# Weights in natural row order, attention output packed whole from a tile by heads, and the clamp on VectorE

## The chip, the cores and the metric

The kernel runs on one core of a Trainium2 chip. The metric is the device time of one execution in microseconds (us). The time before was 523.95 us, the median of three runs (523.85 to 524.45). Engines: PE is TensorE, DVE is VectorE, ACT is ScalarE, POOL is GpSimd; SPq and ACTq are the sequencers of SyncE and ScalarE when they issue transfers. PEld is PE's loading of weights.

A ratio below is the mean time of one kernel's runs over the mean of the other's runs of the same rounds, with a 95% interval. It is therefore not quite the ratio of the medians that are quoted beside it.

## The reference

```python
# attention: B=4, H=8, S=768, D=48
f = 1 / (1 + exp(-f_logit))
for t in range(S):
    state = f[:, :, t, :, None] * state + einsum('bhd,bhe->bhde', k[:, :, t], v[:, :, t])
    y[:, :, t] = einsum('bhd,bhde->bhe', q[:, :, t], state)
x = y.transpose(0, 2, 1, 3).reshape(3072, 384)
# maxout feed-forward: 384 -> 768 -> 384
out = maximum(maximum(x @ w1, x @ w2), x @ w3) @ w_out
```

The four weight matrices come in as float64. The kernel reads them as pairs of 32-bit words and rounds them to fp32 itself.

## The kernel before

The attention goes in 24 units, each one chunk of 64 tokens of two batches, 128 tokens in all. A unit is called chunk *u* here. Four chunks make a group of 512 tokens, and there are six groups. While PE works on the attention of one group, the feed-forward network (FFN) of the group before is slipped in step by step: 18 steps of six matmuls with w1, w2 and w3, then four steps with `w_out`. In the first group, the FFN steps also carry the rounding of the weights, 24 pieces of 128 columns. One rounding is a chain over three engines:

```python
def round_begin(n, h):
    ...
    nc.scalar.activation(top, hi, AF.Abs)                       # ACT
    nc.gpsimd.tensor_scalar(top, top, HI_MIN, None, op0=max)    # POOL: the clamp
    nc.vector.tensor_scalar(top, top, 3, 0x3FFFFFF8, ...)       # DVE: shift and mask
    nc.scalar.activation(rest, lo, AF.Copy, scale=2.0 ** -29)   # ACT
    nc.gpsimd.tensor_tensor(top, top, rest, op=ALU.add)         # POOL
def round_end(n, h):
    nc.vector.scalar_tensor_tensor(w, hi, 0xC0000000, top, ...) # DVE: combine
```

Heads are 48 wide, so 384 features do not fall on 128 partitions head by head. The kernel before puts 48 rows of each of the first six heads at partitions 0 and 64, and fills the 16 rows behind each with a quarter of the last two heads. The weights' rows must be in the same odd order. That costs four transfers for a weight piece:

```python
def in_rows(dst, src):              # two parts of 48 rows and two of 16
    ...
for h in range(2):                  # at the start: 3 pieces x 2 halves x 4 parts = 24 transfers
    for n in range(3):
        load_weight(n, (h,), one)
...
finish(2, xT); pack(2, xT)          # six copies out of PSUM, then six transfers of `last`
load(GRP); load_v(GRP)              # inputs of chunk 4
pairs(3)
for r in rounds[0:3]: round_begin(*r)
values(3)
for r in rounds[0:3]: round_end(*r)
...
finish(3, xT); pack(3, xT, both)
```

`both` means that the transfers alternate between the queues of SP and ACT; otherwise SP issues them.

Of the kernel before, what the change touches and what calls it, by code (L numbers as in the profile page):

```python
# [9 lines left out]
FP32 = mybir.dt.float32  # L10
I32 = mybir.dt.int32
U32 = mybir.dt.uint32
AF = mybir.ActivationFunctionType
ALU = mybir.AluOpType
# [40 lines left out]
def kernel(  # L55
# [28 lines left out]



# [4 lines left out]
    def fast():  # L91
        ctx = ExitStack()
        with ctx:
# [91 lines left out]
            def in_rows(dst, src):  # L185
                parts = []
                for par in range(2):
                    p0 = par * DP
                    parts.append((dst[p0:p0 + D], src[0:NK * 2 * D].rearrange(
                        "(kt par p) c -> par p kt c", kt=NK, par=2)[par]))  # L190
                    parts.append((dst[p0 + D:p0 + DP], src[NK * 2 * D:].rearrange(
                        "(par kt p) c -> par p kt c", par=2, kt=NK)[par]))
                return parts
# [3 lines left out]
            pieces = [(w_in[i][:, :, c0:c0 + 256], src[:, c0:c0 + 256], in_rows)  # L197
                      for c0 in range(0, DFF, 256) for i, src in enumerate((moe_w1, moe_w2, moe_w3))]
            pieces += [(w_out[:, 2 * n:2 * n + 2, :], moe_w_out[n * 256:(n + 1) * 256, :],
                        lambda dst, src: [(dst, src.rearrange("(j p) c -> p j c", p=128))]) for n in range(3)]  # L200
            RAW = 6
            raw = {}

            def half(x, n, h, words=1):
                return x[:, :, h * 128 * words:(h + 1) * 128 * words] if n < 9 else x[:, h:h + 1, :]

            def load_weight(n, halves=(0, 1), queues=both):
                if n >= len(pieces):
                    return
                dst, src, split = pieces[n]  # L210
                words = 1
                if src.dtype != FP32:
                    words = 2
                    a, w = dst.shape[1:]
                    if n not in raw:
                        raw[n] = work.tile([128, 2 * 768], U32, name="raw", bufs=RAW)
                    dst, src = raw[n].rearrange("p (a c) -> p a c", a=a), src.bitcast(U32)
                if len(halves) == 1:
                    c = slice(halves[0] * 128 * words, (halves[0] + 1) * 128 * words)
                    dst, src = dst[:, :, c], src[:, c]  # L220
                for i, (d, s) in enumerate(split(dst, src)):
                    queues[i // 2].dma_start(out=d, in_=s)  # L222

            halfway = {}
            N = 384

            def round_begin(n, h):
                if n in raw:
                    a = pieces[n][0].shape[1]
                    words = half(raw[n].rearrange("p (a c) -> p a c", a=a), n, h, 2)  # L230
                    words = words.rearrange("p a (c two) -> p a c two", two=2)
                    lo, hi = words[:, :, :, 0], words[:, :, :, 1]
                    shape = "p (a c) -> p a c"
                    a = lo.shape[1]



                    top = work.tile([128, N], U32, name="top_bits", bufs=4).rearrange(shape, a=a)
                    nc.scalar.activation(top.bitcast(FP32), hi.bitcast(FP32), AF.Abs)  # L239
                    nc.gpsimd.tensor_scalar(top.bitcast(FP32), top.bitcast(FP32), HI_MIN, None, op0=ALU.max)  # L240
                    nc.vector.tensor_scalar(top, top, 3, 0x3FFFFFF8, op0=ALU.logical_shift_left, op1=ALU.bitwise_and)  # L241

                    rest = work.tile([128, N], U32, name="rest_bits", bufs=3).rearrange(shape, a=a)
                    nc.scalar.activation(rest, lo, AF.Copy, scale=2.0 ** -29)
                    nc.gpsimd.tensor_tensor(top, top, rest, op=ALU.add)  # L245
                    halfway[n, h] = (top, hi)

            def round_end(n, h):
                if n in raw:
                    top, hi = halfway.pop((n, h))  # L250
                    nc.vector.scalar_tensor_tensor(half(pieces[n][0], n, h).bitcast(U32), hi, 0xC0000000, top,
                                                   op0=ALU.bitwise_and, op1=ALU.bitwise_or)
                if h == 1 and n + RAW < len(pieces):
                    raw.pop(n, None)
                    load_weight(n + RAW)


            rounds = [(3 * (j // 2) + i, j % 2) for j in range(NJ) for i in range(3)]
            rounds += [(9 + j // 2, j % 2) for j in range(NJ)]
# [125 lines left out]
            def finish(u, xT):  # L385
# [10 lines left out]
                xT, last = xT  # L396
                t0 = u % GRP * UT
                for par, a, n in ((0, 0, 2), (1, 1, 1), (0, 1, 1)):
                    i, o = slice(par * DP, (par + n) * DP), slice((par ^ a) * DP, ((par ^ a) + n) * DP)
                    nc.scalar.copy(last[o, t0 + a * C:t0 + (a + 1) * C], y[i, a, NK * C:HP * C])  # L400
                for par, a, n in ((0, 0, 2), (1, 1, 1), (0, 1, 1)):
                    i, o = slice(par * DP, (par + n) * DP), slice((par ^ a) * DP, ((par ^ a) + n) * DP)
                    nc.scalar.copy(xT[o, :, t0 + a * C:t0 + (a + 1) * C],  # L403
                                   y[i, a, 0:NK * C].rearrange("p (h t) -> p h t", h=NK))
                ready.pop(u)

            def pack(u, xT, queues=one):

                slot = u % GRP
                if slot < GRP - 2:  # L410
                    return
                xT, last = xT
                t = slice(0 if slot == GRP - 2 else slot * UT, (slot + 1) * UT)
                for i in range(NK):
                    for par in range(2):
                        p0 = par * DP
                        queues[par].dma_start(out=xT[p0 + D:p0 + DP, i, t],
                                              in_=last[p0 + i * TAIL:p0 + (i + 1) * TAIL, t])


            def ffn(g, xT):
                xT = xT[0]
                hm = work.tile([128, NJ, TOK], FP32, name="hm", bufs=1)
                for j in range(NJ):
                    top = None
                    for i in range(3):
# [10 lines left out]
                        if g == 0:  # L437
                            step = 3 * j + i
                            for r in [3 + step] if step < 12 else [2 * step - 9, 2 * step - 8][:24 - 2 * step + 9]:
                                if r < len(rounds):  # L440
                                    round_end(*rounds[r])
                                if r + 1 < len(rounds):
                                    round_begin(*rounds[r + 1])
# [24 lines left out]
            def new_xT():  # L468
                return work.tile([128, NK, TOK], FP32, name="xT"), work.tile([128, TOK], FP32, name="last")
# [4 lines left out]
            with tc.manual_schedule():  # L474
# [4 lines left out]
                load(2, one, "f")  # L479
                load(2, one, "kq")  # L480
                load_v(1)
                load(3)
                load_v(2)
                load_v(3)
                for h in range(2):
                    for n in range(3):
                        load_weight(n, (h,), one)
# [10 lines left out]
                for u in range(2):  # L498
# [5 lines left out]
                    finish(u, xT)  # L504
# [5 lines left out]
                finish(2, xT)  # L510
                pack(2, xT)
                load(GRP)
                load_v(GRP)
                pairs(3)
                for r in rounds[0:3]:
                    round_begin(*r)
                values(3)
                for r in rounds[0:3]:
                    round_end(*r)
                round_begin(*rounds[3])  # L520

                nc.tensor.transpose(ps_tr.tile([128, 128], FP32, name="tr"), ident, ident)
                finish(3, xT)
                pack(3, xT, both)
                for n in range(3, RAW):
                    load_weight(n)
# [7 lines left out]
                load(GRP + 1)  # L534
                load_v(GRP + 1)
                fill(1)
                for u in range(GRP, NU):
# [3 lines left out]
                    if u > GRP:  # L541
                        finish(u - 1, xT)
                        pack(u - 1, xT)
# [25 lines left out]
                finish(NU - 1, xT)  # L569
                pack(NU - 1, xT)  # L570
# [11 lines left out]
    def general():  # L582
# [5 lines left out]
        with ctx:  # L588
# [53 lines left out]
            def chunk(u, xT):  # L642
# [60 lines left out]
                if c < NCH - 1:  # L703
# [10 lines left out]
                    for par in range(2):  # L714
# [6 lines left out]
                        else:  # L721
                            nc.vector.tensor_copy(new, ds[r, :, e])


                z = work.tile([G, H, D], FP32, name="g_z")
                nc.vector.tensor_tensor(z, y.rearrange("t (h d) -> t h d", d=D), own, op=ALU.add)
                x = work.tile([G, NK, 2, DP], FP32, name="g_x")
                nc.vector.tensor_copy(x[:, :, :, 0:D], z[:, 0:2 * NK].rearrange("t (i par) d -> t i par d", par=2))
                nc.vector.tensor_copy(x[:, :, :, D:DP],
                                      z[:, 2 * NK:].rearrange("t par (i d) -> t i par d", d=TAIL))  # L730
                x = x.rearrange("t i par d -> t (i par d)")
# [75 lines left out]
```

## Time and profile before

| stretch of the span (kernel before) | us | what holds it |
|---|---|---|
| to the first FFN matmul | 56.3 | weights issued in 24 transfers, then the pack |
| first FFN matmul to first `w_out` matmul | 84.8 | roundings through POOL |
| the rest | 381.2 | PE, busy without a gap |
| span | 522.3 | |

A row of the table ends where PE starts something that it could not start earlier. A saving in the third row counts only if it is PE's own. A saving in the first two counts if it shortens what PE waits for. The prediction shows the lines.

### The profile page before, as it was taken

Reading aid. Unit: us, or ns where it says so; the run is one execution under the profiler, and the core shown is the slowest. Engines: PE = TensorE matmul, PEld = TensorE weight load, DVE = VectorE, ACT = ScalarE, POOL = GpSimd, SP = SyncE. Lnnn points to the kernel's source line nnn. Section 1 sums busy time; section 2 is a strip of 40 time slices with the busy share of each in tenths; the row PEclk is TensorE's granted clock in tenths of the full one; section 3 lists DMA queues with packets and bytes.
Section 4 is the critical chain, followed back from the end, with each engine's and each line's share of the span. In section 5 each row is a group of like instructions: output and inputs, shape, how many; then the busy total and the mean of one; then the engine's idle time right before and its main releaser. Section 6 shows DMA issues by size and latency. Waiting matters only on the chain.

```text
span 522.3 us, 10050 instructions
## 1 busy us (share of the span) xinstructions
PE 469.9 (90%) x4067; PEld 252.4 (48%) x4067; DVE 209.8 (40%) x322; ACT 120.9 (23%) x299; POOL 126.8 (24%) x156
## 2 busy tenths in 40 slices
PE   5730679997699999999999999999999999999994
PEld 4630334553365555565454654545655445544452
DVE  7733147675632543523553243556225521021110
ACT  2332132552221231131123122202302210200000
POOL 2124158888622121211220220221021210000000
PEclk9785689997799999999999999999999999999998
DMA  9955998773115660126630146711163001200012
GB/s 131 142 157 105 179 163 114 170 132 44 28 33 73 112 79 1 28 53 87 107 50 10 33 67 107 88 18 28 35 83 72 1 4 23 50 0 0 1 23 45
DMA packets 164456, 34.98 MB, mean 67 GB/s; under 512 B 154800, under 2 KB 161328, under 8 KB 164400
## 3 DMA queue, kind: packets, MB, share of 16 engines
q1 hardware_dynamic: 160848, 31.46, 38.2%
q10 hardware_dynamic: 3552, 2.78, 3.1%
q8 instruction: 34, 0.56, 0.5%
q14 instruction: 22, 0.18, 0.1%
HBM read 28.31 MB, written 4.72 MB: 63 GB/s over the span
## 4 chain that ended last, share of the span: by engine, by line
PE 74%; DMA 7%; SPq 6%; POOL 5%; issue 3%; ACT 2%; DVE 1%; ACTq 0%; POOLq 0%; DVEq 0%
PE p L429 47%; PE p L448 18%; SPq L161 3%; DMA raw<-in_moe_w_dram 3%; PE y L393 2%; PE y L365 2%; SPq L222 2%; DMA xT<-last 2%; POOL top_bits L240 2%; POOL top_bits L245 2%; PE a L351 2%; PE y L374 1%; PE tr L338 1%; DMA f_ld<-in_f_logit_dram 1%; DMA k_ld<-in_k_dram 1%
## 5 line engine op out<-in xcount | busy, mean ns | idle before, releaser
L429 PE MATMUL p<-xT,w_in 128*128 128x512 f32 x648 | 295.3, 609 | 13.7 <-DMA xT<-last 12.8
L429 PEld LDWEIGHTS p<-xT,w_in 128*128 128x128 f32 x648 | 122.2, 194 | 155.1 <-issue 149.7
L448 PE MATMUL p<-w_out,hm 128*128 128x384 f32 x288 | 97.5, 497 | 0.0
L448 PEld LDWEIGHTS p<-w_out,hm 128*128 128x128 f32 x288 | 55.3, 194 | 39.2 <-issue 4.5
L435 DVE TENSOR_TENSOR top<-p,top 128x512 f32<-128x512 f32 x36 | 24.9, 690 | 100.3 <-PE p L429 100.3
L433 ACT COPY top<-p 128x512 f32<-128x512 f32 x36 | 21.0, 584 | 180.4 <-PE p L429 164.3
L311 POOL COPY ends<-r 128x8 f32<-128x8 f32 x24 | 4.6, 192 | 184.4 <-DVE r L305 184.4
L435 DVE TENSOR_TENSOR hm<-p,top 128x512 f32<-128x512 f32 x36 | 24.7, 685 | 38.2 <-PE p L429 38.2
L451 ACT COPY o<-p 128x384 f32<-128x384 f32 x24 | 11.5, 478 | 115.1 <-PE p L448 93.4
L354 DVE TENSOR_TENSOR at<-a,mask 128x512 f32<-128x512 f32 x24 | 16.6, 690 | 53.6 <-PE a L351 53.6
L240 POOL TENSOR_SCALAR top_bits<-top_bits 128x384 f32<-128x384 f32 x24 | 28.6, 1191 | 30.5 <-ACT top_bits L239 30.2
L245 POOL TENSOR_TENSOR top_bits<-top_bits,rest_bits 128x384 uint32<-128x384 uint32 x24 | 28.8, 1201 | 13.9 <-DVE top_bits L241 11.2
L319 DVE TENSOR_TENSOR_SCAN prod<-gate,from_inv 128x520 f32<-128x520 f32 x24 | 31.9, 1331 | 0.0
L305 DVE TENSOR_TENSOR_SCAN r<-gate,from_one 128x520 f32<-128x520 f32 x24 | 29.7, 1239 | 2.9 <-issue 2.4
L323 POOL TENSOR_TENSOR qh<-qt,prod 128x512 f32<-128x512 f32 x16 | 18.8, 1178 | 49.0 <-DVE qt L270 49.0
L241 DVE TENSOR_SCALAR top_bits<-top_bits 128x384 uint32<-128x384 uint32 x24 | 8.6, 359 | 44.8 <-POOL top_bits L240 44.8
L393 PE MATMUL y<-qh,state 48*48 48x64 f32 x704 | 15.1, 225 | 10.8 <-DVE st L382 10.8
L365 PEld LDWEIGHTS y<-at,v_ld 64*64 64x64 f32 x768 | 14.2, 141 | 21.3 <-issue 18.4
L365 PE MATMUL y<-at,v_ld 64*64 64x64 f32 x768 | 17.5, 232 | 6.1 <-issue 4.5
L403 ACT COPY xT<-y 64x192 f32<-64x192 f32 (+1 forms) x72 | 22.7, 315 | 1.0
L312 POOL TENSOR_TENSOR kh<-kt,r 128x512 f32<-128x512 f32 x16 | 19.0, 1188 | 14.2 <-DVE kt L270 12.8
L340 ACT COPY ks<-tr 128x512 f32<-128x512 f32 x22 | 12.9, 584 | 40.6 <-PE tr L338 40.6
(65 smaller groups left out, 299.9 us busy)
## 6 DMA issues: line engine op xcount, KB each, us to landing
v_ld<-in_v_dram SPq DMA_DIRECT2D x48, 96.0 KB, 3.3
out_dram<-o SPq DMA_DIRECT2D x48, 96.0 KB, 2.2
raw<-in_moe_w_out_dram SPq DMA_DIRECT2D x3, 768.0 KB, 4.6
f_ld<-in_f_logit_dram SPq DMA_DIRECT2D x32, 64.0 KB, 2.7
k_ld<-in_k_dram SPq DMA_DIRECT2D x32, 64.0 KB, 2.6
q_ld<-in_q_dram SPq DMA_DIRECT2D x32, 64.0 KB, 2.6
raw<-in_moe_w_dram SPq DMA_DIRECT2D x12, 144.0 KB, 3.3
raw<-in_moe_w_dram ACTq DMA_DIRECT2D x6, 288.0 KB, 5.8
```

The source lines that it names most:

```text
L240: nc.gpsimd.tensor_scalar(top.bitcast(FP32), top.bitcast(FP32), HI_MIN, None, op0=ALU.max)
L245: nc.gpsimd.tensor_tensor(top, top, rest, op=ALU.add)
L305: nc.vector.tensor_tensor_scan(r[:, 0:LEN][:, ::-1], flat(gate)[:, ::-1], flat(from_one)[:, ::-1], 1.0, op0=ALU.mult, op1=ALU.max)
L312: (nc.vector if u < BY_ROWS else nc.gpsimd).tensor_tensor(kh.rearrange("p h a t -> p a h t"), kt, by_batch(r[:, 1:LEN + 1].rearrange("p (x ...
L319: nc.vector.tensor_tensor_scan(flat(prod), flat(gate_tiles[u % 2]), flat(from_inv[u % 2]), 1.0, op0=ALU.mult, op1=ALU.max)
L365: nc.tensor.matmul(y[o:o + DP, a, hp * C:(hp + 1) * C], lhsT=v_ld[s, 2 * hp + par, :], rhs=d["at"][s, par, hp, :], start=(hp == 0), stop=F ...
L393: nc.tensor.matmul(y[o:o + D, a, hp * C:(hp + 1) * C], lhsT=st[r, a, hp, :], rhs=d["qh"][r, a, hp, :], start=False, stop=(hp == HP - 1), s ...
L403: nc.scalar.copy(xT[o, :, t0 + a * C:t0 + (a + 1) * C], y[i, a, 0:NK * C].rearrange("p (h t) -> p h t", h=NK))
L429: nc.tensor.matmul(p, lhsT=w_in[i][:, kt, j * 128:(j + 1) * 128], rhs=xT[:, kt, :], start=(kt == 0), stop=(kt == NK - 1))
L433: nc.scalar.copy(top, p)
L435: nc.vector.tensor_tensor(hm[:, j, :] if i == 2 else top, p, top, op=ALU.max)
L448: nc.tensor.matmul(p[:, 0:DM], lhsT=hm[:, j, i * UT:(i + 1) * UT], rhs=w_out[:, j, :], start=(j == 0), stop=(j == NJ - 1))
```

## The change

The intent: let x and w1, w2, w3 keep their natural row order, so that a weight piece is one transfer of 128 rows. Collect the attention's output in a tile by heads, with three copies out of PSUM in place of six. Move it whole into natural order by ten transfers a pack. Move the clamp from POOL to DVE. Spread the roundings evenly over the 18 steps. With this go all weight transfers on SP's queue (ACT issues none) and twelve buffers for raw weights in place of six (`RAW`).

```diff
-    pieces = [(w_in[i][:, :, c0:c0 + 256], src[:, c0:c0 + 256], in_rows) ...]
-    RAW = 6
+    pieces = [(w_in[i][:, :, j * 128:(j + 1) * 128], src[:, j * 128:(j + 1) * 128]) ...]
+    RAW = 12
...
+            nc.sync.dma_start(out=dst, in_=src.rearrange("(a p) c -> p a c", a=a))
...
-    nc.gpsimd.tensor_scalar(top, top, HI_MIN, None, op0=ALU.max)
+    nc.vector.tensor_scalar(top, top, HI_MIN, None, op0=ALU.max)
...
+    heads = keep.tile([128, HP, TOK], FP32, name="heads")
+    # finish: three copies of y into heads[o, :, t] instead of six into xT and last
+def pack(u0, u1, xT, queues=one):
+    for h in range(H):          # eight heads, two of which cross a multiple of 128
+        ...
+            queues[n % 2].dma_start(out=xT[lo % 128:..., lo // 128, t], in_=heads[p0:..., h // 2, t])
...
-    for r in [3 + step] if step < 12 else [2 * step - 9, 2 * step - 8]: ...
+    for r in range(*(3 + (len(pieces) - 3) * n // last for n in (step, step + 1))): ...
...
     load(3)
+    load_weights(3)
     load_v(2); load_v(3)
-    for h in range(2):          # 24 transfers for three weight pieces
-        for n in range(3):
-            load_weight(n, (h,), one)
...
-    finish(2, xT); pack(2, xT); load(GRP); load_v(GRP)
+    finish(2); load_weights(3); load(GRP); load_v(GRP)
+    round_begin(0)
     pairs(3)
...
-    pack(3, xT, both)
+    pack(0, GRP - 1, xT, both)
...
-    pack(u - 1, xT)                       # in the loop, after finish(u - 1)
+    if u % GRP == 3:   pack(0, 2, xT)
+    elif u % GRP == 0: pack(3, 3, xT, both)
```

## The prediction

> **What bounds the kernel now.** I read the page's slices first, then the busy table cut at five moments, then the timeline at the two places where TensorE stands still, then who waits for whom there. In the slices, one slice is 13.06 us.
>
> ```profile
> PE   5730679997699999999999999999999999999994
> PEclk9785689997799999999999999999999999999998
> DMA  9955998773115660126630146711163001200012
> ```
>
> From the twelfth slice on (some 140 us) PE is full and its clock is granted in full until the last slice. Everything this kernel loses lies before that. The windows are cut at the dummy transpose that ends chunk 3's first part (33), the first FFN matmul (56.28), the first matmul with w_out (141.06) and the last FFN group (453). Columns are window, its length, then busy us of PE, PEld, DVE, ACT, POOL, PEclk, DMA share, GB/s.
>
> ```profile
> 0.00:33.00 33.00, 22.57 (x481) 18.43 (x481) 22.51 (x44) 10.54 (x27) 4.68 (x24) 0.90 0.99 144
> 33.00:56.28 23.28, 1.16 (x34) 0.95 (x33) 4.71 (x9) 5.40 (x14) 8.88 (x8) 0.57 0.65 126
> 56.28:141.06 84.78, 72.33 (x652) 38.45 (x652) 48.73 (x80) 32.20 (x73) 59.76 (x60) 0.88 0.73 120
> 141.06:453.00 311.94, 311.94 (x2749) 165.19 (x2746) 125.44 (x177) 66.83 (x175) 53.51 (x64) 0.99 0.33 51
> ```
>
> Row two: 23.3 us in which PE works 1.2. Row three: the first FFN group, whose weights are rounded on the way; 12.5 us idle, and the 72.3 busy are partly at half clock. Row four: PE never idle, so no other engine's saving counts there. The timeline of the second row:
>
> ```profile
> 21.70 14.89 SPq L222 DMA_DIRECT2D raw<-in_moe_w_dram  x24
> ...
> 34.09 0.55 ACT L239 ACTIVATE top_bits<-raw 128x384 f32<-128x384 f32 x1 [2.50 <-DMA raw<-in_moe_w_dram]
> ...
> 36.71 3.80 SPq L417 DMA_DIRECT2D xT<-last  x6
> ...
> 42.33 1.10 PE L393 MATMUL y<-qh,state 48*48 48x64 f32 x32 [9.28 <-DVE st L382]
> ...
> 47.58 9.52 ACTq L222 DMA_DIRECT2D raw<-in_moe_w_dram  x6
> ...
> 56.28 4.79 PE L429 MATMUL p<-xT,w_in 128*128 128x512 f32 x6 [12.84 <-DMA xT<-last]
> ```
>
> The SP queue spends 14.9 us issuing 24 small transfers for three weight pieces. So the first rounding starts at 34.09, and behind it in DVE's order stands chunk 3's state (st), and behind that the matmuls of its output, 9.3 us late. Chunk 4's loads, held up too, are issued just before the pack's last transfers, whose issue starts at 49.17; those take 6.7 us to land and PE starts at 56.28. In row three the waits (waiter, what it waited for, total us, times, longest) are
>
> ```profile
> DVE top_bits L241 <- POOL top_bits L240: 35.3, 18, 17.4
> ...
> ACT top L433 <- DMA raw<-in_moe_w_dram: 16.0, 1, 16.0
> ...
> PE y L365 <- issue: 4.5, 1, 4.5
> PE a L351 <- DVE qh L323: 4.3, 3, 2.0
> ```
>
> POOL is the busiest helper (59.8 of 84.8) and it sits in the middle of each rounding, so DVE, in order, stands behind it and PE behind DVE. The second line is ACT stuck in issuing weight transfers of its own. The 4.5 put down to "issue" is at 134.7: the timeline shows DVE walking through four roundings, each waiting for POOL, before it gets to the mask (at, 138.39) that PE needs.
>
> **What the Trainium skill says.** "DMA: Bandwidth & Descriptors", Rules for kernel authors: use one 128-partition transfer rather than two on disjoint halves, and spreading over queues only saves issue time. The trace agrees in part: SP's issues cost 0.42 to 0.63 us each whatever they carry. "VectorE: DVE Perf Modes", The perf-mode tier table: an fp32 tensor_scalar in SBUF runs at two elements a cycle. The shift (L241, also 4-byte, 384 elements) takes 0.36 us, against 0.55 at the least for the two-input op of that size. "SBUF — State Buffer", SBUF: two separate sides: DVE in such a mode or with two SBUF inputs and GpSimd lock each other out of a shared port pair. POOL's add takes 0.99 us at best and up to 1.92 beside a DVE scan; DVE's combining op 0.54 to 1.17. "TensorE: Matmul & The Clock Gate", Part 1: an idle PE falls to half clock until it has been busy for a while. Here one FFN step of 6 matmuls took 4.79 us after the long idle and 2.66 (half of 5.32 for 12) when warm.
>
> **The change part by part.** (a) Weights: a piece is one transfer of 128 rows of 1 KB runs, 393 KB. 24 issues before the first FFN step become 3 early and 3 more after them. I take SP's order as written and 0.63 us an issue: chunk 3's loads end at 18.9 as now, pieces 0 to 2 go out by 20.9, v of chunks 2 and 3 by 23.5, pieces 3 to 5 by 25.5 (nothing before them waits), chunk 4 by 31. The first w_out pieces, also full 128-partition transfers, moved at 306 to 331 GB/s in 2 us windows, the 48-row weight parts at 170 to 217; so I estimate 1.3 us a piece and have 0 to 2 in place by 26, before ACT is free for them.
>
> (b) Finish: six PSUM copies become three of 256 columns. The existing 64 and 192 columns take 0.21 and 0.315 us, so 256 take some 0.37: 1.1 instead of 1.6 us, and chunk 2's copies end at 31.1. Then ACT does abs and rest for rounds 0 to 3 at 0.45 a start, to about 34.8. DVE: max and shift of round 0 to 32.5, mask (0.69) to 33.2, max and shift of 1 and 2 to 34.6. PE's values from 33.2 to 34.4, DVE st to 35.2, PE's output to 36.0, ACT's copies to 37.2. The round ends come after st, no longer in its way.
>
> (c) Pack: ten transfers (eight heads, two of which cross a multiple of 128) for all four chunks at once, five on each of SP and ACT; at 0.6 and 0.8 us (ACT's three took 2.38) issue ends at 41.2, plus 1.9 to 2.5 to land, as the chunk loads are gone by then: first FFN matmul at 43.5, against 56.28. Gain 12.8 us. 786 KB a group instead of 197 is paid in DMA time that is idle (share 0.33 in row four).
>
> (d) The clamp: 24 times 1.19 us leave POOL (28.6), 24 times 0.36 join DVE (8.6). In the first group 20 roundings begin, so POOL falls from 59.8 to 36, DVE rises from 48.7 to 55.9. It also removes a POOL round trip from the chain of each rounding. Roundings are spread 21 over 18 steps, not one a step for twelve and two a step at the end, which is where the 4.5 us wait arose. ACT no longer issues weights.
>
> First group's PE work at full clock: 72.3 busy less four cold stretches in the timeline (56: 2.1, 75: 2.9, 126: 2.7, pairs and values at 125.6 and 139.2: 1.3) is 63.3. One cold stretch at the start stays (2.2). DVE at 55.9 plus its waits for POOL's add (1.1 us where nothing else stands between shift and combine, say 8 of 21 times, and 0.4 in the others: 14) is as long as PE's 65.5: they alternate, so I add 5 us of mutual waiting. Group: 70.5 us instead of 84.8; gain 14.3.
>
> (e) The rest: 522.3 less 141.1 is 381.2. At 141 PE was cold again: 24 w_out matmuls took 10.17 us, later 7.94. If it arrives warm that is 2.2 less: 379. The part with other groups doesn't change on PE.
>
> Sum: 43.5 + 70.5 + 379 = 493 of span; the time is 1.65 above the span (523.95 less 522.3): 494.7, say 495.
>
> **Rivals.** DVE takes POOL's place: it would have 70 us of work and waits in the first group. For it: the scans and masks of four chunks are already on DVE and its port is shared. Against: it is only 57% busy there now. If it binds fully, the group takes 78 to 80 us, the time is 503 to 505.
> The pack is the new wait: ten transfers instead of six, the longest path 1.1 + 4.0 + 2 = 7.1 us from finish to landing. At a group's change PE reads the new xT 9.4 us after finish (152.33 to 161.75), at the end 7.8 (444.97 to 452.75). So it should fit by a hair at the end; if ACT's issues are slower, 1 us there, and 1 to 2 us at each of four changes: 496 to 505.
> The start is bound by DMA bytes, not by issue: the first 20 us run at a share over 1. If weight pieces and chunk 4's loads queue up before the pack, the first matmul comes at 50 and the time is 501. Against: the share falls to 0.65 in 33 to 56.
> Nothing gained (same): both the start and the group would have to fail, at 514 or more; only if DVE's load were far worse than counted.
>
> **Range and chances.** The firm part is the start and the end of the POOL chain; the uncertain one is the mutual waiting of DVE and PE, 0 to 12 us around my 5, and the landing of the first pack, 3 us either way. Range 487 to 507. The limit for faster by over 2% is 513.5; I give 0.94 for it, 0.05 for within 2%, 0.01 for slower.
>
> **What would show it.** Right: first FFN matmul at 41 to 46; three raw transfers on SP near 19 to 21; the first w_out matmul at 110 to 120; POOL's wait gone from the list of DVE's waits for the shift; PE full from there with no "DMA xT" wait. Wrong: PE waiting for DVE's top or hm by more than 8 us in the first group; PE waiting for DMA xT from heads at later changes of group; the first matmul after 50; PEclk under 0.9 after 50 us.

## The result, and the profile after

The changed kernel took 504.38 us, the median of four runs (503.72 to 505.19). The kernel before took 524.17 us in the same rounds (523.85 to 524.45). The ratio is 0.9623 [0.9607, 0.9640]. The prediction said 495 with a range of 487 to 507. The direction and the range hold, and the middle is 9.4 us too low.

The slices of the changed kernel's page (one slice is 12.57 us):

```profile
PE   5755999996989999999999999999999999999994
...
PEclk9875999998999999999999999999999999999998
DMA  9995996720156612266602276402460011200011
```

The hole in slices three to five is smaller, with digits 5, 5 and 9 where the kernel before had 3, 0 and 6. PE is at nine tenths from the fifth slice on, but for a dent in the tenth slice (113 to 126 us), where its clock is down to 8 tenths and DMA to 0, and a smaller one in the twelfth. The busy table, cut at the corresponding moments (columns as in the prediction: window, length, then PE, PEld, DVE, ACT, POOL, PEclk, DMA share, GB/s):

```profile
33.00:43.29 10.29, 3.27 (x97) 2.73 (x98) 7.46 (x14) 4.83 (x12) 3.99 (x4) 0.62 0.54 88
43.29:121.47 78.18, 71.66 (x663) 37.87 (x663) 56.78 (x104) 30.20 (x64) 37.89 (x42) 0.94 0.70 150
121.47:146.00 24.53, 22.35 (x179) 12.72 (x180) 7.89 (x11) 4.78 (x10) 5.31 (x6) 0.88 0.24 49
146.00:433.00 287.00, 287.00 (x2556) 150.62 (x2555) 114.73 (x162) 53.84 (x113) 46.82 (x56) 1.00 0.38 62
```

The row of 23.3 us in which PE worked 1.2 is now 10.3 us, of which it works 3.3. POOL's busy time from the first FFN matmul to the last rounding is 37.9 us where the kernel before had 59.8, and DVE's is 56.8. From 146 us on PE is full again, as it was before.

The timeline of the start shows the weights and the pack (columns: start, us, engine, line, operation, tiles, count, and in brackets the idle time before and what ended it):

```profile
19.11 1.69 SPq L199 DMA_DIRECT2D raw<-in_moe_w_dram  x3
...
40.00 4.82 SPq L380 DMA_DIRECT2D xT<-heads  x5
40.40 3.21 ACTq L380 DMA_DIRECT2D xT<-heads  x5
...
43.29 2.05 PE L392 MATMUL p<-xT,w_in 128*128 128x512 f32 x2 [4.13 <-DMA xT<-heads]
```

Three weight pieces are issued in 1.7 us in place of 14.9, and the first FFN matmul starts at 43.29 us, where the prediction had 43.5. What is new is in PE's waits between 43 and 150 us (waiter, what it waited for, total us, times, longest):

```profile
PE p L392 <- DMA xT<-heads: 5.1, 2, 4.1
PE p L411 <- DVE w_out L225: 4.3, 2, 2.9
PE p L392 <- ACT o L414: 2.2, 1, 2.2
```

The first line is the pack at the start. The second and third were not in the kernel before. L411 is the matmul with `w_out`, so the second line says that PE stands for the last roundings. Here are these matmuls:

```profile
113.37 2.85 PE L411 MATMUL p<-w_out,hm 128*128 128x384 f32 x8
119.08 0.91 PE L411 MATMUL p<-w_out,hm 128*128 128x384 f32 x2 [2.86 <-DVE w_out L225]
121.47 7.78 PE L411 MATMUL p<-w_out,hm 128*128 128x384 f32 x14 [1.48 <-DVE w_out L225]
```

The first ten take from 113.37 to 121.47. At the rate at which 24 of them run later (8.01 us, so 0.33 each) they need 3.3 us, so 4.8 us are lost. The other fourteen take 7.78 us where 4.7 would do, and another 3.1 us go: the granted clock was 1.00 from 113.37 to 119.08, half of which PE stood, and 0.61 from 121.47 to 129.25. And here is what DVE, which works its queue in order, does just before the second last rounding:

```profile
113.90 0.70 DVE L238 STREAM_TRANSPOSE gate<-sig 128x512 f32<-128x512 f32 x1
114.64 1.58 DVE L273 TENSOR_TENSOR_SCAN r<-gate,from_one 128x520 f32<-128x520 f32 x1
...
117.84 1.18 DVE L225 SCALAR_TENSOR_TENSOR w_out<-raw,top_bits 128x384 uint32<-128x384 uint32 x1
```

The gates of chunk 8 (a transpose, a scan, a reciprocal and another transpose) stand ahead of a rounding for which PE is about to wait. That rounding itself took 1.18 us, the last one (120.86) 0.56; POOL was at work on chunk 8's `kh` from 117.42 to 118.60, beside the slow one.

The third wait, 2.2 us for ACT's `o`, has its origin elsewhere. This is the pack of three chunks on SP, and ACT's part of the pack of the fourth:

```profile
107.20 27.89 SPq L380 DMA_DIRECT2D xT<-heads  x10
...
131.52 3.21 ACTq L380 DMA_DIRECT2D xT<-heads  x5
```

SP's own waits tell why ten transfers took 27.9 us:

```profile
SPq L380 <- DMA xT<-heads: 24.4, 3, 21.7
```

SP stood 21.7 us in the middle of its pack until a transfer of ACT had landed. That transfer belongs to a later pack, which waited for a chunk not yet computed. Behind SP's pack stand the output transfers, which then start at 136.68. ACT cannot copy the next `o` before the older ones are out, and PE waits for ACT at 141.95. The data don't demand any of this. The program as built explains it, and the semaphores in the trace agree (the eighth transfer of SP's pack waits on the semaphore that ACT's first one, issued at 131.52, signals): each transfer signals its landing on one of eight semaphores, given out in turn over both queues in the order in which the builder placed the transfers, and before a semaphore is given out again the issuing queue waits for its last use. In that order ACT's later pack stands inside SP's earlier one:

| place in the order | queue | transfer | semaphore | waits for |
|---|---|---|---|---|
| 129 | ACT | pack of chunk 7, first | 0 | ACT's copies of chunk 7 |
| 131 | SP | pack of chunks 4 to 6, fifth | 2 | its last use |
| ... | both, mixed | | 3 to 7 | |
| 137 | SP | pack of chunks 4 to 6, eighth | 0 | transfer 129 |

### The profile page after: what moved, and what is told of

It reads as the page before. It is cut to its first block, busy times and chain, and to the rows that moved or that the text cites. A ratio compares the mean times of both kernels' runs of the same rounds, so it can differ in the third digit from the quotient of the medians.

```text
span 502.6 us, 9969 instructions
## 1 busy us (share of the span) xinstructions
PE 467.9 (93%) x4067; PEld 250.9 (50%) x4067; DVE 217.2 (43%) x346; ACT 108.7 (22%) x227; POOL 98.7 (20%) x132
## 4 chain that ended last, share of the span: by engine, by line
PE 80%; DVE 6%; DMA 4%; SPq 4%; ACT 1%; issue 1%; POOL 1%; ACTq 0%; DVEq 0%; POOLq 0%
PE p L392 53%; PE p L411 17%; SPq L158 3%; PE y L363 2%; PE y L333 2%; DMA xT<-heads 2%; PE a L319 2%; PE tr L306 2%; PE y L342 1%; DMA v_ld<-in_v_dram 1%; POOL top_bits L217 1%; PE tr L234 1%; DVE top_bits L213 1%; DMA k_ld<-in_k_dram 1%; DVE top_bits L212 1%
## 5 line engine op out<-in xcount | busy, mean ns | idle before, releaser
L392 PE MATMUL p<-xT,w_in 128*128 128x512 f32 x648 | 291.9, 602 | 7.3 <-DMA xT<-heads 5.1
L392 PEld LDWEIGHTS p<-xT,w_in 128*128 128x128 f32 x648 | 120.5, 191 | 147.0 <-issue 134.1
L411 PE MATMUL p<-w_out,hm 128*128 128x384 f32 x288 | 98.8, 501 | 4.3 <-DVE w_out L225 4.3
L411 PEld LDWEIGHTS p<-w_out,hm 128*128 128x128 f32 x288 | 55.5, 195 | 44.7 <-DVE w_out L225 5.6
L217 POOL TENSOR_TENSOR top_bits<-top_bits,rest_bits 128x384 uint32<-128x384 uint32 x24 | 27.2, 1133 | 50.3 <-DVE top_bits L213 27.9
L273 DVE TENSOR_TENSOR_SCAN r<-gate,from_one 128x520 f32<-128x520 f32 x24 | 30.9, 1288 | 2.9 <-issue 2.2
L369 ACT COPY heads<-y 64x256 f32<-64x256 f32 (+1 forms) x72 | 26.6, 369 | 14.3 <-PE y L363 13.3
L297 POOL TENSOR_TENSOR state<-st,ends 128x384 f32<-128x384 f32 x22 | 21.1, 958 | 0.2
L238 DVE STREAM_TRANSPOSE gate<-sig 128x512 f32<-128x512 f32 x16 | 11.3, 708 | 21.2 <-ACT sig L254 21.2
L319 PE MATMUL a<-qh,kh 48*64 48x64 f32 x768 | 16.5, 225 | 0.5 <-DVE qh L291 0.5
```

The source lines that it names most:

```text
L273: nc.vector.tensor_tensor_scan(r[:, 0:LEN][:, ::-1], flat(gate)[:, ::-1], flat(from_one)[:, ::-1], 1.0, op0=ALU.mult, op1=ALU.max)
L297: nc.gpsimd.tensor_tensor(t, states[u % 2], ends[:, u, :].unsqueeze(2).to_broadcast([128, 2 * HP, D]), op=ALU.mult)
L319: nc.tensor.matmul(p[t, par, hp * C:(hp + 1) * C], lhsT=kh[r, hp, a, :], rhs=qh[r, a, hp, :], start=True, stop=True)
L369: nc.scalar.copy(heads[o, :, t0 + a * C:t0 + (a + 1) * C], y[i, a, 0:HP * C].rearrange("p (h t) -> p h t", h=HP))
L392: nc.tensor.matmul(p, lhsT=w_in[i][:, kt, j * 128:(j + 1) * 128], rhs=xT[:, kt, :], start=(kt == 0), stop=(kt == NK - 1))
L411: nc.tensor.matmul(p[:, 0:DM], lhsT=hm[:, j, i * UT:(i + 1) * UT], rhs=w_out[:, j, :], start=(j == 0), stop=(j == NJ - 1))
```

## The experiments

Twelve kernels ran. All gave correct results. They ran in later rounds than the changed kernel, and in those the kernel before took 522.97 to 523.15 us instead of 524.17; so where a run is compared with the changed kernel, the ratios are safer than the medians. "E3" below means the kernel of the third experiment, on which later ones build. L212 and the like are lines of the changed kernel.

### Which part of the change gave what

**e1_clamp_back**: the changed kernel with the clamp on GpSimd again.

```diff
-    nc.vector.tensor_scalar(top, top, HI_MIN, None, op0=ALU.max)
+    nc.gpsimd.tensor_scalar(top, top, HI_MIN, None, op0=ALU.max)
```

> The changed kernel with the clamp put back on GpSimd, everything else new. Theory (POOL's part of the rounding was what held the first FFN group): POOL goes from 37.9 us busy in that group to about 62 of some 75 us, the rounding chain gets its POOL round trip back, the last w_out rounding comes 5 to 10 us later and the time is 509 to 515. Rival (VectorE is the bound now, so the clamp is worth nothing there): 500 to 505, no slower than the changed kernel at 504.4.

Measured: 514.54 us (513.78 to 515.96), ratio to the kernel before 0.984 [0.9811, 0.9869]. The theory holds; POOL is busy for 56.4 us of the group's 75.4. The first FFN matmul comes at 45.35 instead of 43.29 and the first `w_out` matmul at 120.77 instead of 113.37; the waits for roundings of `w_out` are 5.4 us.

**e2_clamp_alone**: the kernel before with nothing changed but the clamp, now on VectorE (the same edit the other way).

> The old kernel with only the clamp moved to VectorE. Theory: the start stays (first FFN matmul at 56 us), the group's PE idle of 12.5 us falls by a third to a half, because ACT and SP are still held by 48 small weight issues: time 516 to 520. Rival (the clamp is the whole gain): 504 to 507. Second rival (the clamp only swaps one busy engine for another): 523 to 525.

Measured: 517.06 us (516.26 to 517.32), ratio 0.9882 [0.9857, 0.9908]. The time is in the theory's range, but not quite by its reasons: the start did not stay, and PE's idle time in the group fell from 12.5 to 10.7 us, by a seventh. The clamp alone gives 1.2%, the rest alone 1.6% (e1), both together 3.8%. So they help each other: in the changed kernel the clamp is worth 10.2 us (514.54 less 504.38), in the kernel before 5.9 (522.97 in the same rounds, less 517.06). By the spans of the profiled runs the difference is smaller, 9.6 against 7.8. The first FFN matmul moves by 2.1 us in either kernel (56.28 to 54.17, 45.35 to 43.29). What differs is the first group (4.3 us in the kernel before, 5.3 in the changed one) and the rest (1.4 and 2.2). These lines show the exchange of the two engines:

```profile
L240 POOL TENSOR_SCALAR top_bits<-top_bits 128x384 f32<-128x384 f32 x24 | 28.6, 1191 | 30.5 <-ACT top_bits L239 30.2
```

```profile
L212 DVE TENSOR_SCALAR top_bits<-top_bits 128x384 f32<-128x384 f32 x24 | 9.4, 392 | 12.0 <-ACT top_bits L211 12.0
```

The first is of the kernel before, the second of the changed one (count, busy us, mean ns). A clamp takes 1191 ns on POOL and 392 ns on DVE.

### The stall of SP

**e3_pack_sp**: the loop's pack of the fourth chunk on SP alone.

```diff
-    pack(3, 3, xT, both)
+    pack(3, 3, xT)
```

> The changed kernel with the pack of the fourth chunk at each change of group on the SP queue alone (the pack before the first group and the one before the last still use both queues). Theory: the 21.7 us for which SP stood still between two transfers of one pack came from a completion semaphore that the program had handed to a later transfer of the ACT queue; with one queue the semaphores go round in issue order, the stall goes, PE's 2.2 us wait for ACT's o copy at the first change of group goes, and the time falls by 1.5 to 3 us to 501.5 to 503. Rival (SP stood still because of the data, chunk outputs or a buffer of xT): the stall stays, 504 to 505. Second rival (ten issues on one queue make the pack late at four changes of group): 505 to 509.

Measured: 502.18 us (500.70 to 503.36), ratio 0.9599 [0.9576, 0.9623]. The theory holds. The same pack now takes this long:

```profile
106.03 6.30 SPq L380 DMA_DIRECT2D xT<-heads  x10
```

The wait for `o` is gone from PE's list, and the waits for `w_out` (2.88 and 1.48 us) are still there. So taking a second queue away removes the wait of 2.2 us that the stall had cost: from the first `w_out` matmul to the end it is 386.8 us (499.0 less 112.2) instead of 389.2. The times alone show it less well: the medians differ by 2.2 us, but they are of different rounds, the ratios differ by 0.0024 (1.3 us), and their intervals overlap.

### The late roundings

**e5_pace15**: E3 with the roundings spread over 15 of the 18 steps, so that they end earlier.

```diff
-    for r in range(*(3 + 21 * n // 18 for n in (step, step + 1))):
+    for r in range(*(min(24, 3 + 21 * n // 15) for n in (step, step + 1))):
```

> e3_pack_sp with the 21 roundings of the first FFN group spread over 15 of its 18 steps instead of all 18, so that the last w_out piece is rounded some 9 us earlier. Theory (the 10 us by which the rest ran longer than predicted are the wait for the last w_out roundings, 4.4 us, the half clock that follows it, 3 us, and the SP stall, 2.2 us): both waits on DVE w_out go, the clock stays full at the first w_out matmuls, the time falls by 5 to 8 us to 494 to 497. Rival (VectorE is full over the whole group, so the debt only moves forward): PE waits for top and hm grow by as much, time 500 to 503.

Measured: 500.70 us (499.98 to 500.79), ratio 0.9573 [0.9549, 0.9597]. This is mostly the rival. The waits for `w_out` are gone and all 24 matmuls run at full clock in 8.01 us, but the first of them comes only at 119.09:

```profile
119.09 8.01 PE L412 MATMUL p<-w_out,hm 128*128 128x384 f32 x24
```

From the first FFN matmul to it the group takes 75.7 us instead of E3's 69.7. The rest after it is 379.1 (498.2 less 119.1), just what the prediction had. The work that had been late was moved forward into steps where PE waits for it too: besides the pack, PE stands for 5.1 us in the group (1.2 in E3), nearly all for DVE; the 2.1 of them that the profile puts down to ACT end with DVE's mask at 85.90.

**e6_half**: E3 with the clamp of every other piece on GpSimd.

```diff
-    nc.vector.tensor_scalar(top, ...)
+    (nc.gpsimd if n % 2 else nc.vector).tensor_scalar(top, ...)
```

> e3_pack_sp with the clamp of every other piece on GpSimd (12 on each engine). If VectorE's load is what makes the w_out roundings late, taking 10 clamps of 0.36 us off it in the group brings them 3 us earlier and the time to 498 to 500. If the round trips through GpSimd are what costs (each adds 1.2 us in a chain that VectorE waits for in order), the time rises to 505 to 508, half way to the kernel with all clamps on GpSimd.

Measured: 504.47 us (503.49 to 505.69), ratio 0.9645 [0.9619, 0.9671], which lies between the two expectations, nearer to the second. Sharing the clamps is worse than giving all of them to DVE. The waits for `w_out` are 5.1 us and the first FFN matmul comes 2.7 us later than in E3.

**e11_no_clamp**: E3 without the clamp. It is not a usable kernel: tiny weights would come out wrong, though the comparison with the reference still passed.

```diff
-    nc.vector.tensor_scalar(top, top, HI_MIN, None, op0=ALU.max)
```

> e3 with no clamp at all: weights below the clamp's limit come out wrong, on purpose, to see what 24 clamps of 0.36 us (21 of them, 7.6 us, in the first group) still cost on VectorE. Theory: from 43 to 125 us VectorE's order is the limit, the 4.3 us of waits for w_out roundings included, so taking 7.6 us of work away gives 6 to 9 us: 493 to 496 against e3's 502.18. Rival: VectorE is 73 per cent busy there, what counts is the chain of each rounding and not its sum of work: 499 to 501.5.

Measured: 491.89 us (490.35 to 493.45), ratio 0.9391 [0.9365, 0.9417]. This is 10.3 us below E3 by the medians (7.3 by the spans of the two profiled runs), at or beyond the theory's end. One wait of 1.1 us for `w_out` remains, and the second block of 24 `w_out` matmuls starts at 122.12 instead of 129.32. So DVE's work in the first group does cost time, about microsecond for microsecond (20 clamps are begun in it, of 0.39 us each, together 7.8), although DVE is busy for only 73% of that time (56.8 of 78.2 in the changed kernel). This run cannot say whether the sum matters or the place of the work; it also makes the chain of each rounding one step shorter.

**e12_order**: no work removed. The start is that of e10 (below). The gates of chunk 8 are put behind the last two roundings, and POOL's six memsets of padding, which had delayed an add of a rounding by 2.1 us, a chunk later.

```diff
-    fill(1); after(n); fill(1); values(u)
+    fill(2 if u == 7 else 1); after(n); fill(0 if u == 7 else 1); values(u)
...
-    if n in (5, 7): pad_blocks(n // 2 % 2)
+    if n in (5, 8): pad_blocks(n > 5)
```

> e10, with two things moved out of the way of the last roundings, and no work removed: the scan and transposes of chunk 8 (3.4 us on VectorE) behind the last two roundings in place of ahead of them, and GpSimd's six memsets of padding (3.4 us) from chunk 6's end to chunk 7's. Theory: in the changed kernel, e3 and e10 the w_out matmuls stood for the roundings of w_out (2.9 and 0.7 to 1.5 us) and then ran at half clock because of the order of work on VectorE and GpSimd, not because of its sum. Then the waits for w_out fall under 1 us, the first 24 w_out matmuls take 8 to 9 us (e10: 15.0), and the time is 492 to 495 against e10's 498.96. Rival: the sum of VectorE's work is what counts (e11), so what is moved is waited for later, by the matmuls of chunk 8 that need its gates: 497 to 499.5.

Measured: 492.13 us (491.90 to 492.96), ratio 0.9406 [0.9388, 0.9423]. The time is at the theory's lower end. The first `w_out` matmuls, the last rounding, and a new line in PE's waits:

```profile
108.12 8.39 PE L411 MATMUL p<-w_out,hm 128*128 128x384 f32 x24
```

```profile
111.12 0.56 DVE L225 SCALAR_TENSOR_TENSOR w_out<-raw,top_bits 128x384 uint32<-128x384 uint32 x1 [1.17 <-POOL top_bits L217]
```

```profile
PE a L319 <- POOL qh L291: 1.5, 1, 1.5
```

All 24 run without a wait in 8.39 us, where the changed kernel took 15.9 (113.37 to 129.25). The last rounding ends at 111.7, before PE gets to it. The rival has a good part of the truth: PE now waits 1.5 us for chunk 8's `qh` and the next 24 take 9.70 us, 1.7 above full clock. So of the 7.9 us that the changed kernel lost at its first 24 matmuls, 7.5 are gone and 3.2 have come back a little later. Against e10 the time is 6.8 us lower by the medians and 3.8 by the spans of the profiled runs; why e10's other runs are slower than its profiled one is open (below). What the order of the gates gave and what the memsets gave was not separated. This is the best of the usable kernels here, 12 us below the changed one.

### The transfers at the start

**e4_four_parts**: the changed kernel with every weight piece in four transfers of 32 rows, all on SP.

```diff
-    nc.sync.dma_start(out=dst, in_=src)
+    for p0 in range(0, 128, 32):
+        nc.sync.dma_start(out=dst[p0:p0 + 32], in_=src[p0:p0 + 32])
```

> The changed kernel with each weight piece sent in four transfers of 32 rows, same bytes, same rows of 1 KB, all on SP. Theory (issue time on the queue is what the one transfer saved): the three early pieces take 12 issues, v of chunks 2 and 3 goes out 5 us later, the next three pieces and chunk 4 behind that, the first FFN matmul comes at 48 to 54 us instead of 43.3 and the time is 509 to 515. Rival (bytes and runs, not issues, set the landing): first FFN matmul at 43 to 45, time 504 to 506.

Measured: 520.80 us (517.91 to 522.24), ratio 0.9936 [0.9896, 0.9975]. The time is worse than both expectations: nearly the whole gain is gone. The first FFN matmul, at 53.50, is where the theory had it, but not for its reason. PE's output of chunk 3, on which the pack waits, comes only 2.5 us later (40.60 instead of 38.05). The rest shows in SP's timeline:

```profile
36.55 9.35 SPq L158 DMA_DIRECT2D f_ld<-in_f_logit_dram  x2
```

Two small transfers of chunk 4 take 9.35 us, 8.1 of them waiting for ACT's part of the pack, by the same shared semaphores. So SP's part of the pack begins only at 50.48. The test that was meant to measure issues had measured a stall.

**e8_first_split**: E3 with only the first three pieces in four transfers each.

> e3_pack_sp with only the three early pieces sent in four transfers each (12 issues for 3), all later pieces whole. Theory: e4_four_parts lost 16 us in two ways, 9 more issues of 0.6 us ahead of v of chunk 2 (2 to 3 us later at the first FFN matmul) and a semaphore of the ACT queue's pack in which chunk 4's load stood still for 8 us; here the program gives no transfer ahead of the pack such a semaphore, so only the first is left: time 504 to 506, first matmul at 44 to 46. Rival (the number of issues alone cost the 16 us): 512 or more.

Measured: 500.47 us (500.11 to 501.32), ratio 0.9565 [0.9541, 0.9589]. Both expected times were wrong: nothing is lost against E3. The first FFN matmul does come later, as the theory said (45.21 against 42.52), but then six run through in 5.46 us, where E3's wait another 1.1 us for the second half of the pack; both end that step near 50.

**e9_four_sp**: e4 with all packs but the last on SP, so that no SP transfer can stand behind one of ACT's.

> Every weight piece in four transfers as in e4, but all packs except the tail's are issued by SP alone, so that no SP transfer can stand behind one of ACT's. Theory: e4's loss against the changed kernel (16.4 us) came mainly from the 9.4 us that SP stood in chunk 4's loads behind ACT's part of the pack. Then the first FFN matmul comes at 45 to 47 (e4: 53.5) and the time is 505 to 509. Rival: the small transfers themselves cost it, during the group too (e4's group took 75.9 us against 69.7 in e3): 512 to 517.

Measured: 510.47 us (507.64 to 513.10), ratio 0.9748 [0.9712, 0.9785], just above the theory's range. Of e4's loss of 16.4 us against the changed kernel, 10.3 are gone. The first FFN matmul comes at 45.81, as the theory said. The remaining 8.3 us against E3 are a loss by the small transfers: 3.3 at the start, and in the group, which takes 80.2 us instead of E3's 69.7, PE waits 8.4 us for the `f_ld` of chunks whose loads stand in SP's queue behind the weight pieces. The profiled run was the slowest of the six (513.10 us), so these figures are at the upper end; and e9 differs from E3 in a second thing, the first pack on SP alone.

**e7_start**: E3 with chunk 2's `v` ahead of the weights and the first rounding behind chunk 3's mask, since PE had waited 2.3 us for the one and 2.7 for the other.

```diff
-    load_weights(3); load_v(2); load_v(3)
+    load_v(2); load_weights(3); load_v(3)
...
-    round_begin(0); pairs(3); round_begin(1)
+    pairs(3); round_begin(0); round_begin(1)
```

> e3_pack_sp with v of chunk 2 issued ahead of the first three weight pieces and the first rounding begun after, not before, chunk 3's mask. The changed kernel's chain shows PE waiting 2.3 us (0.9 in e3) for v of chunk 2, behind 1.2 MB of weights, and 2.7 us for the mask that stands behind the first clamp and shift in VectorE's order. Theory (the start is a chain and nothing else holds it): first FFN matmul 3 to 4 us earlier, at 39 us, time 498 to 499.5. Rival (the landing of the weights, or the chunk loads, come up right behind): 0 to 1 us, 501 to 502.5.

Measured: 499.28 us (498.14 to 500.92), ratio 0.9547 [0.9520, 0.9574]. The time is as expected, the way is not. PE's output of chunk 3 comes at 34.24, 3.0 us earlier than in E3, but the first FFN matmul only at 43.98, because SP's loads of chunk 4 wait 2.8 us for ACT's part of the pack and SP's part starts at 40.50.

**e10_start_sp**: e7 with the first pack on SP alone.

```diff
-    pack(0, GRP - 1, xT, both)
+    pack(0, GRP - 1, xT)
```

> e7's order of the start, and the first pack on SP alone. Theory: in e7 chunk 4's v loads stood on SP until 39.12 behind ACT's part of the pack, so SP's part began only at 40.50. With one queue the pack begins when the copies end, at 36.5, its ten issues end at 42.8, and as the transfers are in the order in which the matmuls need them the first FFN matmul comes at 40 to 41.5 (e7: 43.98): 496 to 498 against e7's 499.28. Rival: ten issues on one queue are simply longer than five on each of two, and the first FFN step ends when it did (49.4): 499 to 500.

Measured: 498.96 us (495.45 to 499.60, seven runs), ratio 0.9540 [0.9516, 0.9564]. The profile shows what the theory said: the pack starts at 36.44 and the first FFN matmul at 39.87. The time doesn't: the median is 0.3 us below e7's, within the intervals. The profiled run was among the two fastest (496.35 us), so its trace may not stand for the other five, and what became of the earlier start in those is open.

## Why the prediction was right or wrong

| part of the time | before | predicted | changed kernel | e12 |
|---|---|---|---|---|
| to the first FFN matmul | 56.3 | 43.5 | 43.3 | 40.5 |
| to the first `w_out` matmul | 84.8 | 70.5 | 70.1 | 67.6 |
| the rest of the span | 381.2 | 379 | 389.2 | 382.6 |
| outside the span | 1.65 | 1.65 | 1.7 | 1.8 |

The table uses the profiled runs (504.31 us for the changed kernel, 492.49 for e12).

**Steps (a) to (c), the start, were right in the sum and right for less good reasons in part.** The first matmul came 0.2 us from the predicted moment. Two errors offset each other within it: PE's output of chunk 3 ended at 39.15 instead of 36.0, because PE waited 2.3 us for `v` and 2.7 for the mask behind the first rounding, while the first matmul came 2.9 us after the last copy (40.36) where the prediction had 6.3. It needs only the first part of the pack; for the rest there was a second wait, of 1.0 us, up to 46.34. The working put most of the gain on the number of transfers. The runs give it less: split in four and free of the stall, the weights cost 3.3 us at the start of some 13 (e9), and splitting the first three pieces costs the kernel no time (e8). One reading behind this was too narrow: 0.42 to 0.63 us are medians of SP's issues by line, and single issues of weights took from 0.31 to 1.75 us. The clamp brings 2.1 of the 13 (e1, e2). That the remaining 8 come from the new order of work and the single pack is argued from this, not shown by a run. Nor is e9's split into four equal parts quite the 48 and 16 rows of the kernel before.

**Step (d), the group, was right in direction and, partly by luck, in size.** The clamp's move was the right mechanism: up to the last rounding POOL was busy for 37.9 us against 36 predicted, DVE for 56.8 against 55.9, with 9.4 us of clamps on DVE against 8.6. The group took 70.1 us against 70.5. But the prediction's group ends where PE reaches `w_out`, and there the row reads (columns as above):

```profile
43.29:113.37 70.08, 67.90 (x653) 36.13 (x653) 50.16 (x93) 30.20 (x64) 34.53 (x38) 0.93 0.78 168
```

When PE reached `w_out`, 6.6 us of DVE's 56.8 were thus not yet done. PE stood for 2.2 us and not for the 5 of mutual waiting (1.0 of the 2.2 was for the pack), and it was busy for 67.9 us and not 65.5, with the clock at 0.53 from 43.29 to 53.00; the two errors offset each other. With all roundings ahead of `w_out` the group takes 75.7 us (e5). The first rival, DVE in POOL's place at 78 to 80 us, was thus nearer than the table shows; the working had itself put DVE's work and waits at 55.9 and 14, together 69.9, and called this as long as PE's 65.5. Of the group's 14.7 us of gain the clamp gives 5.3 (e1's group takes 75.4). The other 9.4 come with the rest of the change: with pieces in four transfers the group takes 75.9 (e4) and 80.2 us (e9), so whole pieces count here too, but no run takes the even spacing or the twelve buffers away alone.

**Step (e), the rest, failed.** The prediction said: "If it arrives warm that is 2.2 less: 379. The part with other groups doesn't change on PE." It was 389.2, by 10.2 more. Three terms make up nearly all of this: 4.8 us lost while PE stood for roundings of `w_out`, 3.1 at a lower clock after it (0.61), and 2.2 at the change of group behind SP's stall, together 10.1. Each was tested. e3 takes the last away, and its rest is 386.8, 2.4 less. e5 takes all three away, and its rest is 379.1, but its group is 6.0 us longer than E3's. e12 takes them away without removing work, and its rest is 382.6: 3.6 above 379, of which 3.2 are chunk 8's `qh` and the cold matmuls behind it. What failed was the assumption that the roundings are done when PE comes to need them. The prediction counted how much work DVE has in the group, and not what stands ahead of the last rounding in DVE's queue. It had read the matching fault in the kernel before (four roundings ahead of chunk 7's mask), and had taken the even spacing as its cure. The amount matters as well as the order: for the 7.9 us lost at the first 24 `w_out` matmuls, e12's new order pays 3.2 elsewhere, and e5's early roundings 6.0.

**The rivals.** The pack as a new wait: at the first change of group PE did wait, but for `o`, not for `xT`, and not because ten transfers are slow; a transfer of one queue stood behind one of another. The start bound by bytes: not to 50 us, the first matmul came when predicted; but PE's 2.3 us for chunk 2's `v` are a wait behind three weight pieces of 393 KB, so bytes had a part in it. At the end of the kernel the pack fits: PE goes on at 433.14 without a wait. Of the signs named, "PE full from there" after the first `w_out` matmul did not come, and "PEclk under 0.9 after 50 us", a sign of being wrong, did (the tenth slice, and 0.61 from 121.47 to 129.25). Both point to the failed step.

## What to carry to other kernels

An engine that is 73% busy can still set the time, by what stands ahead of the one instruction that another engine is about to need: look at the order of its queue at the hand-over, since moving 3.4 us of DVE's work behind the last roundings, and as much of POOL's out of their way, gained 6.8 us here by the medians and 3.8 by the profiles (e10 to e12), with no work removed. Removing 7.8 us of DVE's work in the group gained 10.3 and 7.3 (E3 to e11), so the amount counts too. When a second queue is added for transfers, ask of every transfer which earlier one it must wait for, data or not; at the change of group one queue in the order of need was better here than two (e3). And when a test of one cost comes out far beyond all expectations, as e4 did, read its trace before believing its number.

## What the Trainium skill lacked or had wrong

- No page has it that transfers of different queues can be tied by a small set of completion semaphores given out in turn. In "DMA: Bandwidth & Descriptors", Rules for kernel authors, several queues only save issue time; here the second queue cost time. SP stood 21.7 us behind ACT's transfer, and the same pack on one queue took 6.3 us instead of 27.9 (e3). It did this again in e4 (8.1 us) and e7 (2.8 us).
- "GPSIMD Engine Reference", 4.1 Engine selection, says that GpSimd is about half as fast as VectorE for two-input operations and roughly at line rate for one-input ones. Here a one-input maximum over 128 by 384 fp32 elements took 1191 ns on GpSimd and 392 on VectorE, a third of it. The measured ratio decides for an operation of this size, and the move paid some 10 us of 514.5 (e1); no run here separates a fixed cost per instruction from the rate.
